# Attention, experts and MLP in one kernel: k's features shifted by a subtraction in some thirds, their maximum negated by a flag in the others, products of zeros at the start

## The chip, the core and the metric

The kernel runs on one core of a Trainium2 chip. The core has five engines with a queue of instructions each: TensorE (PE; its weight loads are listed as PEld), VectorE (DVE), ScalarE (ACT), GpSimd (POOL) and SyncE (SP, here used to issue DMAs). The metric is the device time of one launch in microseconds, the median of several runs. Three runs of the kernel before took 1137.62, 1134.53 and 1134.76 us; the median is 1134.76.

## The reference, cut to what matters

Three layers follow each other: an attention without softmax over 4 batches, 8 heads, 576 tokens and 64 columns; a mixture of 8 experts with the best 2 of each token; an MLP with a leaky ReLU. All is in 32-bit floats. The change touches only the features phi of the attention:

```python
def phi(x):                                            # q or k: (4, 8, 576, 64)
    proj = np.einsum('bhsd,df->bhsf', x, w_phi)        # (..., 128)
    proj = proj - np.max(np.abs(proj), axis=-1, keepdims=True)
    return np.concatenate([np.exp(proj), np.exp(-proj)], axis=-1)
q_p, k_p = phi(q), phi(k)
kv = np.einsum('bhsf,bhsd->bhfd', k_p, v)
num = np.einsum('bhsf,bhfd->bhsd', q_p, kv)
den = np.einsum('bhsf,bhf->bhs', q_p, k_p.sum(2))[..., None] + 1e-06
x = num / den                                          # then experts, then MLP
```

With m the largest absolute value of a row, the features are exp(proj - m) and exp(m - proj).

## The kernel before

Attention works on 16 pairs of heads (`i` from 0 to 15), one after the other. Each pair has 9 tiles of 128 rows for q and 9 for k, taken in thirds of 3 tiles (`c` = 0, 1, 2). A third goes through these steps. The raw rows are split into a high and a low 16-bit part: ScalarE makes the high part, GpSimd the low part (`split_one`, lines 303 and 304), and a DMA on SP transposes both (line 306). For the first arrays that would take too long, so `split_pe` does the split in thirds (lines 317, 318) and transposes on TensorE (line 323) with a copy by ScalarE (line 325). `proj` multiplies by w_phi into a PSUM bank `pj` (lines 333, 334). There are four such banks for all projections and transposes of both q and k; one that is asked for is waited for until its last reader is done. VectorE takes the largest absolute value of each row (line 336).

For q, VectorE then subtracts that maximum (line 343), which frees the bank; TensorE transposes the result (`q_transpose`, line 360), and ScalarE takes both exponentials of a whole third in two instructions (line 364). For k, VectorE negates the maximum (line 339), and ScalarE takes the exponentials straight from the bank with the maximum or its negative as a bias for each row. The bias is one number per partition, so there are six instructions, one per tile and sign (`k_exp`, line 352), and the bank is held until the last of them. Products of k's features with v follow (`kv`, line 374), a copy (line 382), a product that folds the routing's weights in (`fold_mm`, line 388) with its copy (line 392), and at the next pair the products with q's features (`num`, recorded at line 211).

The order is written out by hand: every engine works in the order in which the code issues. The body of the loop for pair i issues the first third of q, the last transposes of pair i-1, the first half of `kv` with half of `num` of pair i-1 between its products, then k's first third of pair i+1 and q's second; then the splits for pair i+2 and, in odd pairs, the loads for later ones; then the second half of `kv`, k's second third of pair i+1 (`proj("k", i + 1, 1)`, line 945), q's third third, the exponentials of k's second third (line 949), the fold, k's last third and its exponentials. Routing work of batches that are done is issued in small pieces in between (`flow`, `site`). Before the loop stand the splits of pair 0 and 1 and k's thirds of pair 0 (lines 826 to 854); `make_fold` puts eight copies of a unit matrix into the routing's weights for `fold_mm`. After attention come the expert products (`mm1`, line 1003, and `mm2`, line 1049) and the MLP with the same lines.

Of the kernel before, what the change touches and what calls it, by code (L numbers as in the profile page):

```python
# [7 lines left out]
F32 = mybir.dt.float32  # L8
F32R = mybir.dt.float32r
F16 = mybir.dt.float16  # L10
BF16 = mybir.dt.bfloat16
I32 = mybir.dt.int32
ACTF = mybir.ActivationFunctionType
ALU = mybir.AluOpType
AX = mybir.AxisListType.X
# [11 lines left out]
def attention_moe_mlp_kernel(  # L27
# [24 lines left out]
    nc = tc.nc  # L52
    B, H, S, D = q.shape
    F = w_phi.shape[1]
# [15 lines left out]
    const = ctx.enter_context(tc.tile_pool(name="const", bufs=1))  # L70
# [38 lines left out]
    def make_split_w_phi():  # L109
        nc.vector.tensor_scalar(out=ident, in0=iota[:, 0:128], scalar1=tokid[:, 0:1],  # L110
                                scalar2=None, op0=ALU.is_equal)
        nc.vector.tensor_copy(ident16, ident)
        nc.scalar.activation(wph, wphi, ACTF.Copy)
        nc.vector.tensor_tensor(out=wpl, in0=wphi, in1=wph, op=ALU.subtract)
# [41 lines left out]
    sm_p = att.enter_context(tc.tile_pool(name="sm", bufs=3))  # L156
# [12 lines left out]
    def make_ones(i, eng):  # L169


        eng.memset(vs[i][:, :, :, D:D + 1], 1.0)
        eng.memset(vs[i][64:128, :, 4], 0.0)
        eng.memset(vs[i][0:64, :, 9], 0.0)

    def make_pads():

        for t in qTs:
            nc.gpsimd.memset(t[:, :, :, NW:], 0.0)

    def make_fold():
        for h in range(H):
            nc.vector.tensor_copy(fr[:, h, 0:D + 1], ident[0:D + 1, 0:D + 1])
# [8 lines left out]
    ks_t = {}  # L192
    raw, stk, qT, qs_t, kvsb, fold, xb = {}, {}, {}, {}, {}, {}, {}
    nA, nB, ke = {}, {}, {}
    nb = ps_a.tile([128, 512], F32, name="nb")
# [7 lines left out]
    def pj(shape, dt, name):  # L203

        npj[0] += 1
        if npj[0] % 4 == 0:
            return ps_c.tile(shape, dt, tag="pj", name=name)
        return ps_a.tile(shape, dt, tag="pj", name=name, bufs=3)
# [82 lines left out]
    def raw_rows(nm, i):  # L291
        t = raw[nm, i // 2]
        if i % 2:
            raw.pop((nm, i // 2))
        return t[:, i % 2]

    def split_one(nm, i, eng=None, cuts=(0, NW)):

        r = raw_rows(nm, i)
        s = spl_p.tile([128, NW, 2, D], F16, tag="spl" + nm, name="spl" + nm)  # L300
        x = spl_p.tile([128, NW, 128], F16, tag="stk" + nm, name="stk" + nm, bufs=3)
        for w in map(slice, cuts, cuts[1:]):
            nc.scalar.activation(s[:, w, 0], r[:, w], ACTF.Copy)
            (eng or nc.gpsimd).tensor_tensor(out=s[:, w, 1], in0=r[:, w], in1=s[:, w, 0],
                                             op=ALU.subtract)
            nc.sync.dma_start_transpose(out=x[:, w], in_=s[:, w].rearrange("p w c d -> p (w c d)"))
        stk[nm, i] = x
# [20 lines left out]
    def proj(nm, i, c):  # L328

        x = stk[nm, i]  # L330
        p = pj([128, 3, F], F32, "pj")
        for t in range(3):
            nc.tensor.matmul(p[:, t], x[:, 3 * c + t], wpl, start=True, stop=False)
            nc.tensor.matmul(p[:, t], x[:, 3 * c + t], wph, start=False, stop=True)  # L334
        m = sm_p.tile([128, 3], F32, tag="m", name="m")
        nc.vector.tensor_reduce(out=m, in_=p, axis=AX, op=ALU.max, apply_absolute_value=True)  # L336
        if nm == "k":
            n = sm_p.tile([128, 3], F32, tag="n", name="n")
            nc.vector.tensor_scalar(out=n, in0=m, scalar1=-1.0, scalar2=None, op0=ALU.mult)
            ks_t[i, c] = p, n, m  # L340
            return
        s = sm_p.tile([128, 3, F], F32, tag="shq", name="shq", bufs=3)
        nc.vector.tensor_tensor(out=s, in0=p, in1=m.unsqueeze(2).to_broadcast([128, 3, F]),
                                op=ALU.subtract)
        qs_t[i, c] = s

    def k_exp(i, c):
        p, *shift = ks_t.pop((i, c))
        e = feat_p.tile([128, 3, 2, F], F32, tag="ke", name="ke", bufs=7)
        for t in range(3):  # L350
            for sg in range(2):
                nc.scalar.activation(e[:, t, sg], p[:, t], ACTF.Exp, scale=1.0 - 2.0 * sg,
                                     bias=shift[sg][:, t:t + 1])
        ke[i, c] = e

    def q_transpose(i, c):
        s = qs_t.pop((i, c))
        p = pj([128, 3, 128], F32, "tq")
        for t in range(3):
            nc.tensor.transpose(out=p[:, t], in_=s[:, t], identity=ident)  # L360
        if c == 0:
            qT[i] = qTs[i % 2]
        for sg in range(2):
            nc.scalar.activation(
                qT[i][:, sg, :, 3 * c:3 * c + 3].rearrange("p h w c -> p w h c"),
                p.rearrange("p w (h c) -> p w h c", h=2), ACTF.Exp, scale=1.0 - 2.0 * sg)
# [12 lines left out]
    def kv_evac(i, h):  # L379
        if h == 0:  # L380
            kvsb[i] = sm_p.tile([D + 1, 2, 2, F], F32, tag="kvs", name="kvs", bufs=2)
        nc.scalar.activation(kvsb[i][:, h], kv_of[:, :, h], ACTF.Copy)  # L382
# [333 lines left out]
    t = 0  # L716
# [102 lines left out]
        nc.vector.tensor_tensor(out=lo, in0=p, in1=hi.bitcast(F32), op=ALU.subtract)  # L819


    def take(g, n):
        for _ in range(n):
            next(g)
# [10 lines left out]
    load_q(1)  # L835
    load_v(0, 1)
    make_split_w_phi()
    make_ones(0, nc.gpsimd)
    k0 = split_pe("k", 0, nc.vector)
    take(k0, 6)  # L840
    q0 = split_pe("q", 0, nc.gpsimd)
    take(q0, 3)
    for c in range(2):
        proj("k", 0, c)
    k_exp(0, 0)
    take(q0, 1)
    k_exp(0, 1)
    take(q0, 2)
    load_gates()
    k1 = split_pe("k", 1, nc.gpsimd)  # L850
    take(k1, 3)
    split_one("q", 1)
    proj("k", 0, 2)
    make_fold()

    todo = {}

# [28 lines left out]
    for i in range(NPAIR + 1):  # L886
        nx, now, before = i + 1 < NPAIR, i < NPAIR, i > 0

        def run(place):
            for f in todo.pop((i, place), []):  # L890
                f()

        if i == NPAIR:
            att_c.close()
            ps_e = ctx.enter_context(tc.tile_pool(name="ps_e", bufs=1, space=PSUM, side="right"))
        run(0)
        first = num(i - 1, 0, 1, 2) if before else []
        second = num(i - 1, 3, 4) if before else []
        if now:
            proj("q", i, 0)  # L900
            if before:
                q_transpose(i - 1, 2)
            site(14)
            kv(i, 0, first)
            site(6, pe=True)
            kv_evac(i, 0)
            q_transpose(i, 0)
            if i == 0:
                k_exp(0, 2)
                take(k1, 3)  # L910
                split_one("k", 2)
                load_k(1, 1)
                for part in range(3):
                    load_v(1, part)
            if nx:
                proj("k", i + 1, 0)
            proj("q", i, 1)
            if nx:
                k_exp(i + 1, 0)
        else:  # L920
            for f in first:
                f()
        if before:
            x_evac(i - 1, 0)
        run(1)
        if i == 0:
            for n in range(1, NV):
                make_ones(n, nc.gpsimd)
            make_pads()
        if 0 < i < NPAIR - 2:  # L930
            split_one("k", i + 2)
        if i + 2 < NPAIR:
            split_one("q", i + 2)
        if i % 2 and (i + 3) // 2 < NPAIR // 2:
            load_double((i + 3) // 2)
        if i == 1:
            load_noise()
            make_constants()
        run(2)
        if now:  # L940
            kv(i, 1, second)
            site(3, pe=True)
            kv_evac(i, 1)
            if nx:
                proj("k", i + 1, 1)
            q_transpose(i, 1)
            proj("q", i, 2)
            if nx:
                k_exp(i + 1, 1)
            site(6)  # L950
            fold_mm(i, 0)
            fold_mm(i, 1)
            if nx:
                proj("k", i + 1, 2)
                k_exp(i + 1, 2)
            else:
                q_transpose(i, 2)
            if before:
                x_evac(i - 1, 1)
        else:  # L960
            for f in second:
                f()
        site(8, pe=True)
        run(3)
        if before:
            for d in (qT, fold):
                d.pop(i - 1)
        if now:
            for c in range(3):
                ke.pop((i, c))  # L970
# [278 lines left out]
    for bi in range(2, NB - 1):  # L1249
        s0 = steps.index((bi, 0))  # L1250
        kind, _, tiles, _ = blocks[bi + 1]
# [78 lines left out]
```

## Time and profile before

| | |
|---|---|
| median of three runs | 1134.76 us |
| the profiled execution | 1134.95 us |
| its span, first to last instruction | 1132.8 us |
| TensorE busy | 1082.2 us, 96% |
| VectorE busy | 725.4 us, 64% |
| ScalarE busy | 574.1 us, 51% |
| GpSimd busy | 219.2 us, 19% |
| granted clock of TensorE, mean | 0.993 |

All but the row of the median come from one profiled execution. Busy time is an average over parts of the run with different limits: attention takes about the first 240 us, and there all engines but SP have work; after that TensorE is busy nearly without a gap. Times in the rows are microseconds from the start of the span, and a line such as L339 is line 339 of the kernel. [...]

### The profile page before, as it was taken

The numbers are of one execution on the slowest core, as the hardware profiler recorded it, in microseconds if no ns is written. First come the engines' busy times: TensorE is split into PE (matmuls) and PEld (weight loads), VectorE is DVE, ScalarE is ACT, GpSimd is POOL, SyncE is SP. The second block draws the span as 40 slices with busy tenths as digits, with TensorE's granted clock in tenths as the row PEclk, the third lists the DMA queues.
The fourth block names the chain that finished last, engine by engine and source line by source line (L and its number), as shares of the span: only waits on it lengthen the run. The fifth ranks groups of instructions, "written<-read, shape, count | busy, mean of one in ns | idle before, by whom it ended". The sixth has DMA issues, their size and how long they took to land. (4 is left out here: it accounts for less than half of the span.)

```text
span 1132.8 us, 18373 instructions
## 1 busy us (share of the span) xinstructions
PE 1082.2 (96%) x6767; PEld 950.4 (84%) x6767; DVE 725.4 (64%) x1555; ACT 574.1 (51%) x1276; POOL 219.2 (19%) x251
## 2 busy tenths in 40 slices
PE   6999989989999999999999999889999999999998
PEld 5888988978888988888888888778888888888886
DVE  4668686878387767676667666576545645645443
ACT  6776766644455444444444454555444444444443
POOL 4211111124334315141413130330000000000000
PEclk9999999999999999999999999999999999999999
DMA  5645554634567646464546362202003003001001
GB/s 142 129 112 142 122 130 107 193 110 156 182 215 249 213 126 199 149 204 143 188 121 210 118 208 80 101 0 94 1 1 112 1 1 109 3 1 29 10 1 37
DMA packets 117003, 125.87 MB, mean 111 GB/s; under 512 B 61040, under 2 KB 87696, under 8 KB 116912
## 3 DMA queue, kind: packets, MB, share of 16 engines
q1 hardware_dynamic: 110320, 104.13, 32.0%
q0 software_dynamic: 6272, 20.03, 5.1%
q8 instruction: 54, 0.88, 0.3%
q10 hardware_dynamic: 320, 0.52, 0.1%
q14 instruction: 37, 0.30, 0.1%
HBM read 96.71 MB, written 19.40 MB: 102 GB/s over the span
## 5 line engine op out<-in xcount | busy, mean ns | idle before, releaser
L1003 PE MATMUL m<-xth,w0l 128*128 128x304 f32 (+5 forms) x800 | 268.3, 335 | 3.3 <-issue 3.3
L1003 PE MATMUL m<-xth,w0h 128*128 128x304 f32 (+5 forms) x800 | 264.9, 331 | 0.0
L1003 PE MATMUL m<-xtl,w0h 128*128 128x304 f32 (+5 forms) x800 | 264.0, 330 | 0.0
L1049 PE MATMUL o<-w1l,hh 128*128 128x512 f32 (+1 forms) x608 | 241.0, 396 | 1.7 <-POOL w1l L752 1.7
L1049 PE MATMUL o<-w1h,hh 128*128 128x512 f32 (+1 forms) x608 | 240.4, 395 | 0.0
L1049 PE MATMUL o<-w1h,hl 128*128 128x512 f32 (+1 forms) x608 | 239.5, 394 | 0.9 <-DVE hl L1007 0.9
L1003 PEld LDWEIGHTS m<-xth,w0l 128*128 128x128 f32 x800 | 150.7, 188 | 16.9 <-issue 3.7
L1003 PEld LDWEIGHTS m<-xtl,w0h 128*128 128x128 f32 x800 | 150.9, 189 | 13.8
L1003 PEld LDWEIGHTS m<-xth,w0h 128*128 128x128 f32 x800 | 150.8, 189 | 10.4
L1049 PEld LDWEIGHTS o<-w1h,hh 128*128 128x128 f32 (+1 forms) x608 | 112.8, 186 | 28.7
L1049 PEld LDWEIGHTS o<-w1h,hl 128*128 128x128 f32 (+1 forms) x608 | 113.0, 186 | 25.6 <-DVE hl L1007 1.4
L1049 PEld LDWEIGHTS o<-w1l,hh 128*128 128x128 f32 (+1 forms) x608 | 113.0, 186 | 23.8 <-POOL w1l L752 2.2
L1013 DVE SCALAR_TENSOR_TENSOR g<-g 128x512 f32<-128x512 f32 (+1 forms) x80 | 53.5, 669 | 110.5 <-ACT g L1012 110.4
L374 PE MATMUL kv<-ke,vs 128*65 128x128 f32 x640 | 121.2, 282 | 2.7 <-ACT kvs L382 1.9
L1012 ACT ACTIVATE g<-m 128x512 f32<-128x512 f32 (+1 forms) x80 | 44.4, 555 | 132.1 <-PE m L1003 131.8
L749 ACT ACTIVATE w1h<-w2r 128x512 fp32r<-128x512 f32 x88 | 55.4, 630 | 88.8 <-PE o L1049 51.1
L1007 DVE SCALAR_TENSOR_TENSOR hl<-m,hh 128x304 fp32r<-128x304 f32 (+4 forms) x128 | 57.9, 470 | 56.8 <-ACT hh L1006 56.6
L752 DVE TENSOR_TENSOR w1l<-w2r,w1h 128x512 fp32r<-128x512 f32 x72 | 49.7, 690 | 60.2 <-ACT w1h L749 59.2
L1016 DVE TENSOR_TENSOR hl<-g,hh 128x512 fp32r<-128x512 f32 (+1 forms) x80 | 51.1, 639 | 52.4 <-ACT hh L1015 49.4
L336 DVE TENSOR_REDUCE m<-pj 128x3 f32<-128x384 f32 x96 | 52.9, 551 | 48.5 <-PE pj L334 46.8
L1006 ACT ACTIVATE hh<-m 128x304 fp32r<-128x304 f32 (+4 forms) x128 | 50.5, 417 | 64.9 <-PE m L1003 62.2
L1015 ACT ACTIVATE hh<-g 128x512 fp32r<-128x512 f32 (+1 forms) x80 | 47.1, 589 | 68.4 <-DVE g L1013 68.4
(189 smaller groups left out, 1810.9 us busy)
## 6 DMA issues: line engine op xcount, KB each, us to landing
w1r<-in_moe_w_dram SPq DMA_DIRECT2D x44, 512.0 KB, 4.8
w2r<-in_moe_w_dram SPq DMA_DIRECT2D x44, 512.0 KB, 4.2
y<-y_dram SPq DMA_DIRECT2D x18, 512.0 KB, 4.9
raw<-in_moe_w_in_dram SPq DMA_DIRECT2D x16, 512.0 KB, 4.3
raw<-in_moe_w_out_dram SPq DMA_DIRECT2D x16, 512.0 KB, 3.8
rawk<-in_k_dram SPq DMA_DIRECT2D x16, 256.0 KB, 3.6
vs<-in_v_dram SPq DMA_DIRECT2D x32, 128.0 KB, 4.3
x_dram<-xb SPq DMA_DIRECT2D x4, 1024.0 KB, 5.0
```

Of the source, the lines that this page charges most:

```text
L336: nc.vector.tensor_reduce(out=m, in_=p, axis=AX, op=ALU.max, apply_absolute_value=True)
L374: nc.tensor.matmul(kv_of[:, sg, h], vs[i // 2 % NV][:, i % 2, 5 * h + n], ke[i, t // 3][:, t % 3, sg], start=(n == 0), stop=(n == 4))
L749: nc.scalar.activation(hi, src, ACTF.Copy)
L752: (nc.gpsimd if pool else nc.vector).tensor_tensor(out=lo, in0=src, in1=hi.bitcast(F32), op=ALU.subtract)
L1003: nc.tensor.matmul(p, w[:, kk], x[:, kk, c0:c1], start=(kk == 0 and m == 0), stop=(kk == KD - 1 and m == 2))
L1006: nc.scalar.activation(hh[:, c0:c1], p, ACTF.Relu)
L1007: nc.vector.scalar_tensor_tensor(out=hl[:, c0:c1], in0=p, scalar=0.0, in1=hh[:, c0:c1].bitcast(F32), op0=ALU.max, op1=ALU.subtract)
L1012: nc.scalar.activation(g, p, ACTF.Copy)
L1013: nc.vector.scalar_tensor_tensor(out=g, in0=g, scalar=0.01, in1=g, op0=ALU.mult, op1=ALU.max)
L1015: nc.scalar.activation(hh[:, c0:c1], g, ACTF.Copy)
L1016: nc.vector.tensor_tensor(out=hl[:, c0:c1], in0=g, in1=hh[:, c0:c1].bitcast(F32), op=ALU.subtract)
L1049: nc.tensor.matmul(acc[n][0:rows], a[:, c], w, start=(f == 0 and m == 0), stop=(f == nf - 1 and m == 2))
```

## The change

Three things change in the attention part, and nothing behind it.

- For k, the thirds of pairs 0 and 1 and the second third of every later pair now go the way of q: VectorE subtracts the maximum into a tile in SBUF (`shk`, two buffers), and ScalarE takes the exponentials of the whole third from there in two instructions. The first and last third of pairs 2 to 15 keep their six exponentials, but the negated maximum is made by a maximum over one element with the negate flag, in place of a multiplication by -1.
- A tile of zeros, 128 by 512 in 16 bits, is filled by VectorE at the start, and TensorE multiplies zeros by zeros: nine products ahead of the first transposes and five more, one or two at a time, before the loop. They write into the bank `nb`, which the first pair's results use only later.
- `make_fold` moves from before the loop to behind the exponentials of k's last third of pair 0, and the transposes of pair 1's k move from there to ahead of the first transposes of q.

```diff
         nc.vector.tensor_reduce(out=m, in_=p, axis=AX, op=ALU.max, apply_absolute_value=True)
-        if nm == "k":
+        if nm == "k" and i > 1 and c != 1:
             n = sm_p.tile([128, 3], F32, tag="n", name="n")
-            nc.vector.tensor_scalar(out=n, in0=m, scalar1=-1.0, scalar2=None, op0=ALU.mult)
+            nc.vector.tensor_reduce(out=n, in_=m.unsqueeze(2), axis=AX, op=ALU.max, negate=True)
             ks_t[i, c] = p, n, m
             return
-        s = sm_p.tile([128, 3, F], F32, tag="shq", name="shq", bufs=3)
+        s = sm_p.tile([128, 3, F], F32, tag="sh" + nm, name="sh" + nm, bufs=3 if nm == "q" else 2)
         nc.vector.tensor_tensor(out=s, in0=p, in1=m.unsqueeze(2).to_broadcast([128, 3, F]),
                                 op=ALU.subtract)
-        qs_t[i, c] = s
+        if nm == "q":
+            qs_t[i, c] = s
+        else:
+            ks_t[i, c] = s,
...
         p, *shift = ks_t.pop((i, c))
         e = feat_p.tile([128, 3, 2, F], F32, tag="ke", name="ke", bufs=7)
-        for t in range(3):
+        for sg in () if shift else range(2):
+            nc.scalar.activation(e[:, :, sg], p, ACTF.Exp, scale=1.0 - 2.0 * sg)
+        for t in range(3) if shift else ():
             for sg in range(2):
...
+    zeros = const.tile([128, 512], BF16, name="zeros")
+
+    def warm(n):
+
+        for _ in range(n):
+            nc.tensor.matmul(nb, zeros[:, 0:128], zeros, start=True, stop=True)
+
...
     make_split_w_phi()
+    nc.vector.memset(zeros, 0.0)
+    warm(9)
     make_ones(0, nc.gpsimd)
     k0 = split_pe("k", 0, nc.vector)
...
     k_exp(0, 0)
+    warm(1)
     take(q0, 1)
     k_exp(0, 1)
+    warm(1)
     take(q0, 2)
     load_gates()
     k1 = split_pe("k", 1, nc.gpsimd)
     take(k1, 3)
     split_one("q", 1)
+    warm(2)
     proj("k", 0, 2)
-    make_fold()
+    warm(1)
...
             kv_evac(i, 0)
+            if i == 0:
+                take(k1, 3)
             q_transpose(i, 0)
             if i == 0:
                 k_exp(0, 2)
-                take(k1, 3)
+                make_fold()
```

## Rows read from the trace of the kernel before

**Rows 1.** The page's part 4: the chain that ended last, by line
```profile
PE m L1003 16%; PE o L1049 16%; PE t L815 1%; DVE y L794 1%; ACT w0h L749 0%; DVE g L1013 0%; DVE w0l L752 0%; DVE xtl L819 0%; ACT w1h L749 0%; ACT xth L818 0%; DVE xg L797 0%; DVE yo L1054 0%; ACT yo L1056 0%; ACTq L1063 0%; ACT hh L1015 0%
```

**Rows 2.** What TensorE waited for, 28 to 240 us: total, times, longest
```profile
PE pj L333 <- ACT ke L352: 7.7, 6, 1.7
PE tq L360 <- ACT ke L352: 2.2, 2, 1.4
PE pj L333 <- DVE shq L343: 1.9, 3, 0.8
...
PE tq L360 <- DVE n L339: 1.7, 1, 1.7
PE tq L360 <- DVE shq L343: 1.5, 3, 0.7
PE pt L656 <- DVE hot L648: 1.2, 1, 1.2
```

**Rows 3.** Timeline of VectorE around one end of a pair: start, us, what
```profile
65.55 0.56 DVE L336 TENSOR_REDUCE m<-pj 128x3 f32<-128x384 f32 x1 [1.31 <-PE pj L334]
66.14 1.28 DVE L339 TENSOR_SCALAR n<-m 128x3 f32<-128x3 f32 x1
67.33 0.54 DVE L336 TENSOR_REDUCE m<-pj 128x3 f32<-128x384 f32 x1
67.91 0.56 DVE L343 TENSOR_TENSOR shq<-pj,m 128x384 f32<-128x384 f32 x1
68.39 0.55 DVE L336 TENSOR_REDUCE m<-pj 128x3 f32<-128x384 f32 x1
```

**Rows 4.** Instructions of lines 339, 343: ns min/median/max, first and last start
```profile
L339 DVE TENSOR_SCALAR n<-m x48: 168/169/1321, 7.9 to 223.5; 128x3 f32<-128x3 f32 x48
L343 DVE TENSOR_TENSOR shq<-pj,m x48: 556/557/559, 13.3 to 234.5; 128x384 f32<-128x384 f32 x48
```

**Rows 5.** Timeline of GpSimd, two of its splits
```profile
12.85 1.56 POOL L318 TENSOR_TENSOR splk<-rawk,splk 128x192 f16<-128x192 f32 x3 [1.48 <-ACT splk L317]
...
66.11 1.28 POOL L304 TENSOR_TENSOR splq<-rawq,splq 128x576 f16<-128x576 f32 x1
```

**Rows 6.** Timeline of TensorE at the same end of a pair
```profile
69.16 0.22 PE L333 MATMUL pj<-wpl,stkq 128*128 128x128 f16 x1 [1.74 <-ACT ke L352]
...
69.49 0.50 PE L360 MATMUL tq<-ident,shq 128*128 128x128 f32 x3
```

**Rows 7.** Stretches: us; PE, PEld, DVE, ACT, POOL busy (count); PEclk, DMA, GB/s
```profile
12.40:16.90 4.50, 4.50 (x24) 4.50 (x23) 1.38 (x5) 1.44 (x5) 2.79 (x4) 1.00 0.45 99
16.90:20.30 3.40, 1.18 (x14) 0.87 (x13) 0.00 (x0) 3.35 (x11) 0.00 (x0) 1.00 0.46 87
20.30:23.70 3.40, 3.40 (x24) 3.40 (x23) 2.64 (x4) 1.85 (x6) 2.00 (x6) 0.51 0.02 5
163.70:166.70 3.00, 1.52 (x20) 1.40 (x18) 2.93 (x8) 2.56 (x9) 1.19 (x1) 1.00 0.64 122
166.70:170.50 3.80, 3.80 (x25) 3.80 (x24) 3.28 (x15) 2.65 (x9) 0.00 (x0) 0.56 0.34 63
```

**Rows 8.** Timeline of ScalarE after the first kv
```profile
17.33 0.87 ACT L364 ACTIVATE qT<-tq 128x384 f32<-128x384 f32 x2
18.09 0.37 ACT L352 ACTIVATE ke<-pj,n 128x128 f32<-128x128 f32 x1
...
19.58 1.30 ACT L325 ACTIVATE stkk<-tr 128x384 f16<-128x384 f16 x3
```

**Rows 9.** Timeline of TensorE at the start
```profile
5.33 1.14 PE L323 MATMUL tr<-ident,splk 128*128 128x128 f16 x9 [5.33 <-DVE splk L318]
...
12.40 4.47 PE L374 MATMUL kv<-ke,vs 128*65 128x128 f32 x20
...
24.70 0.22 PE L333 MATMUL pj<-wpl,stkk 128*128 128x128 f16 x1
```

**Rows 10.** Groups by line, VectorE: count, busy us, mean ns, idle before
```profile
L119 DVE MEMSET ones<- 128x128 bf16 x1 | 0.2, 165 | 0.0
```

## The prediction

> **What bounds the kernel now.** I read the chain of waits first. [rows 1] There the reader is to see that the chain that ends last is TensorE nearly throughout and lies in the two expert and MLP products, lines 1003 and 1049. The change touches nothing there: it can only let that stretch begin earlier or later, so every microsecond won or lost in the attention stretch (the first 240 us) goes through to the end. So I next asked what TensorE waits for inside attention. [rows 2] These six rows add up to 7.7 + 2.2 + 1.9 + 1.7 + 1.5 + 1.2 = 16.2 us between 28 and 240 us. Almost all of it stands at one place, once in each head pair: the end of the pair, where pair i hands over to pair i+1. The timeline of one such place [rows 3] shows why, on VectorE: the maximum of k's second third begins at 65.55, its negation takes 1.28 us for three numbers per partition, and q's maximum and subtraction, and k's last third, queue behind it. Over all 48 negations the median is 169 ns and the longest 1321 ns [rows 4]. The long ones are those that start beside a GpSimd split: here the split of q runs from 66.11 to 67.39 and the negation ends at 67.42 [rows 5]. TensorE pays twice [rows 6]: the first projection of the next pair waits 1.74 us (69.16) for the bank that ScalarE's six exponentials of that third still read, and the transposes of q's last third follow at 69.49. At the start a third view matters, the stretches by granted clock [rows 7].
>
> **Second third of k by subtraction (pairs 2 to 15, 14 handovers).** Removed: a negation and six exponentials from PSUM. Added: one subtraction on VectorE and two exponentials of 384 columns. The subtraction's price is that of q's, 556 to 559 ns in all 48 [rows 4]; in a queue the next instruction starts about 0.08 us before it has ended, so it takes 0.48. A maximum takes 0.56 and its successor starts 0.58 after it. So the new handover is: k's maximum, subtraction, q's maximum, subtraction = 0.58 + 0.48 + 0.58 + 0.56, plus 0.06 until TensorE starts: q's transposes start 2.26 us after k's maximum. The bank of k is free after 0.58 + 0.56, before the next pair's first projection wants it (TensorE's own work from its projection of k to q's transposes takes about 2.6 us from 0.54 us before the maximum, so 2.06 us after it, and 2.26 ends last). In [rows 3, 6]: 65.55 + 2.26 = 67.81 instead of 69.49, a gain of 1.68. What is late next there is VectorE's subtraction of q, by 0.2 us, not a bank.
>
> The same subtraction for every handover, each from the start of the maximum of k's second third to the start of q's transposes: 39.77 to 42.26 (gain 0.23), 52.31 to 55.29 (0.72), 65.55 to 69.49 (1.68), 79.49 to 82.41 (0.66, and 0.36 that TensorE then waits for the fold copy, which comes earlier with ScalarE's shorter work: 1.02), 93.74 to 96.98 (0.98), 121.97 to 124.95 (0.72), 135.21 to 138.73 (1.26), 150.28 to 153.19 (0.65), 163.31 to 166.99 (1.42), 179.21 to 182.84 (1.37), 193.46 to 196.98 (1.26), 207.13 to 210.12 (0.73), 220.23 to 223.36 (0.87); of these 13 pairs of rows one stands, in [rows 3, 6]. At 108.03 routing work stands between: there the two table rows on VectorE end 0.71 earlier, and I count 0.71. Sum 13.6 us. The upper end is the whole of [rows 2], less the 0.4 at 28 us and 0.5 at 235 us that are no such handover: 15.3. The lower end: if the subtraction too were held until GpSimd's split ends, it would start when the negation now ends; q's subtraction would end 0.47 later than now, and the same list gives 3.0. I take 13.6, since the 48 subtractions show no long one, the first of them (13.30 us) beside GpSimd's splits from 12.85 [rows 4, 5].
>
> [...]
>
> **The negate flag (first and last thirds).** The negation becomes a maximum over one element each. No such row exists; the bounds are 169 ns of the old form and 540 ns of a maximum over 128 columns [rows 4, 3], and I take 0.17, as start-up cost makes up most of both for so few numbers. These thirds have their negation at the median, clear of GpSimd; no wait goes and none comes: 0. If it cost 0.54, the last third's sits behind q's subtraction, off TensorE's path, and ScalarE would begin it 0.4 later, with the fold copy in front of it already done. So 0 in both cases.
>
> **ScalarE.** Two exponentials of 384 columns cost as q's pair, 0.87 [rows 8]; six cost 1.5 (18.09 to 19.58). That is 0.6 us per third, 12 us over 20 thirds, but TensorE sees it only through banks and the fold copy, which are counted above, and through the start, below.
>
> [...]
>
> **The start.** The zero fill stands on VectorE ahead of k's split, and the first nine zero products on TensorE ahead of the first transposes, which began at 5.33 [rows 9]. The fill is four times the 128-column memset of 165 ns [rows 10] at most, 0.66; the products can then start at about 5.4, where the split's end put the transposes. [...] From there to the first kv it was 7.07 us, nearly all ScalarE in one chain; k's first two thirds take 4 x 0.435 there instead of 12 x 0.25, 1.26 less, and the projections at full clock 0.3 less: kv starts at 14.75. In front of it stand five more zero products, hidden while ScalarE is the chain. It is half as long if the clock is up, 2.24, and ends at 17.0, against 16.87 now; if the clock isn't up, the projections and fillers take 1.25 more and it ends at 20.4. Is it up? [...] I take it as up.
>
> After the first kv, now: copy of kv, q's pair, six exponentials, three copies of the next k, and k's second third of pair 1 is projected at 24.70 [rows 8, 9], 7.83 after kv's end. New: copy 0.4, three copies 1.3, q's pair 0.87, half a pair of exponentials, then the rest of the second kv, which waits for them: 4.15. Of the 3.7 us won, 1.7 is the clock, which is 0.51 in 20.3 to 23.7 now [rows 7]. The fold's copies move behind all this on VectorE and are needed 2 us later. The start gains 24.70 - 21.15 = 3.55 if the clock holds. It fell now after 16.9 to 20.3 with TensorE busy 1.18 of 3.40 us, and after 163.7 to 166.7 with 1.52 of 3.00 [rows 7]. New it is busy some 1.5 of 3 after the first kv, like the second of these rows, so I take one more fall, half of 3.4 us: 1.7. The start is worth 1.85, with ends 3.55 and, with the clock not up and a fall behind it, a loss of 1.55.
>
> **The fall at 166.7.** The 1.5 us gap in front of it is one of the handovers that close. 3.8 us at 0.56 lose 1.65 [rows 7]; it should go. Ends 0 and 1.65; I take 1.65, because with a 0.2 us gap that stretch looks like the others, at 1.00.
>
> **Sum.** 13.6 + 1.85 + 1.65 = 17.1. The profiled execution took 1134.95 (span 1132.8 and 2.15 around it), 0.2 above the median shown: 1134.95 - 17.1 = 1117.85, and I predict 1117.8.
>
> **Rivals.** (1) Half of the handover gain turns into a new wait: the loads of the pair after next, which SP issues at the handovers, come in at the same time while ScalarE's split comes 1.7 us earlier. For it: six handovers carry such loads. Against: no ScalarE wait for a load among the rows, and q's load lands about 1.3 us before the earlier split would ask. It gives 1134.95 - 6.8 - 1.85 = 1126. Chance 0.14. (2) The change doesn't do what it says, and the subtraction is held like the negation: handovers 3.0, start and fall nothing: 1132. Against it the 559 ns. Chance 0.07. (3) The zeros don't raise the clock: 13.6 + 1.65 - 1.55 = 13.7, 1121; for it, that only real products have raised it in the trace. Chance 0.10. (4) Slower: the late start is never paid back. [...] Chance 0.04. The forecast keeps 0.65, with its own range 1113 to 1124 (15.3 and both clock terms at their best at one end; 11 and no clock term at the other).
>
> **Range and chances.** A change under 0.3%, 3.4 us, can't be told from none. Faster by more needs under 1131.4: forecast, (1), (3) and a part of (2), 0.92; same 0.04; slower 0.04. The range 1112 to 1129 takes in (1) and (3) and leaves out (2) and (4).
>
> **What would show it.** Right: no negation of k above 0.2 us after the first pairs; waits of TensorE at projections and q's transposes between 28 and 240 us down from 16 to about 3; the handover 2.3 us from k's maximum to q's transposes; attention ending some 17 us earlier and the rest unchanged. Wrong: subtractions of 1 us; TensorE's first kv ending after 18; a new releaser at the handovers; clock of 0.5 between 17 and 24 twice.

## The result and the profile after

The changed kernel took 1118.0 us (median of 4 runs, 1117.33 to 1120.06), the kernel before beside it 1136.19 us (4 runs, 1134.53 to 1137.89). The ratio is 0.9843, with a 95% interval of 0.9819 to 0.9866: 1.6% faster. The profiled execution took 1117.33 us with a span of 1115.3, so against the profiled execution of before the difference is 17.6 us in time and 17.5 in span.

The chain that ended last is still TensorE in the two expert and MLP products (lines 1022 and 1068 are 1003 and 1049 of before), as in [rows 1]:

```profile
PE m L1022 17%; PE o L1068 16%; PE t L820 1%; DVE y L799 1%; ACT w0h L754 0%; DVE g L1032 0%; DVE w0l L757 0%; DVE xtl L824 0%; ACT w1h L754 0%; ACT xth L823 0%; DVE xg L802 0%; DVE yo L1073 0%; ACTq L1082 0%; ACT yo L1075 0%; ACT hh L1034 0%
```

What TensorE waited for between 26 and 230 us of the kernel after (total, times, longest), which answers to [rows 2]:

```profile
PE kv L379 <- ACT kvs L387: 3.3, 2, 2.2
PE tq L365 <- DVE shq L343: 2.8, 3, 1.4
PE pt L661 <- DVE hot L653: 1.0, 2, 0.5
PE o L1068 <- DVE hl L1026: 0.9, 1, 0.9
```

The reader is to see that the two rows on `ke` (7.7 and 2.2 us), the row on `n` and the projections' row on `shq` are gone: no bank of k is waited for any more. The first two rows that are left stand at a few pairs each; the first is the subject of kernels e5 and e6.

VectorE at the end of the pair that [rows 3] showed, in the kernel after (start, us, what):

```profile
60.07 0.56 DVE L336 TENSOR_REDUCE m<-pj 128x3 f32<-128x384 f32 x1 [1.38 <-PE pj L334]
60.66 0.56 DVE L343 TENSOR_TENSOR shk<-pj,m 128x384 f32<-128x384 f32 x1
61.14 0.55 DVE L336 TENSOR_REDUCE m<-pj 128x3 f32<-128x384 f32 x1
61.72 0.56 DVE L343 TENSOR_TENSOR shq<-pj,m 128x384 f32<-128x384 f32 x1
```

TensorE's transposes of q's last third follow at 62.42, 2.35 us after the first row (before: 65.55 to 69.49, 3.94). Four rows of instructions with their durations (ns min/median/max), where [rows 4] had the old ones: the sign change, k's new subtraction, k's new exponential, which reads SBUF, and beside it q's, which reads PSUM:

```profile
L339 DVE TENSOR_REDUCE n<-m x28: 155/156/157, 30.3 to 208.7; 128x3 f32<-128x3 f32 x28
...
L343 DVE TENSOR_TENSOR shk<-pj,m x20: 557/557/558, 10.9 to 205.6; 128x384 f32<-128x384 f32 x20
...
L354 ACT ACTIVATE ke<-shk x40: 506/522/543, 11.5 to 206.6; 128x384 f32<-128x384 f32 x40
...
L369 ACT ACTIVATE qT<-tq x96: 470/491/537, 17.8 to 220.2; 128x384 f32<-128x384 f32 x96
```

TensorE at the start, which answers to [rows 9]:

```profile
5.23 3.81 PE L832 MATMUL nb<-zeros 128*128 128x512 bf16 x9 [5.23 <-DVE zeros L850]
8.88 0.67 PE L323 MATMUL tr<-ident,splk 128*128 128x128 f16 x9
...
14.01 2.35 PE L379 MATMUL kv<-ke,vs 128*65 128x128 f32 x20
...
21.12 0.22 PE L333 MATMUL pj<-wpl,stkk 128*128 128x128 f16 x1
```

The nine transposes took 0.67 us here and 1.14 before, and ahead of them TensorE had nothing but products of zeros: so in this run these zeros alone had brought the clock to its upper level.

The stretches after the first kv, and the one that answers to the fall at 166.7 in [rows 7]; the columns are those of that group, and the granted clock stands third from the end:

```profile
16.20:19.60 3.40, 2.78 (x33) 2.09 (x31) 3.30 (x11) 3.21 (x9) 1.36 (x2) 1.00 0.26 44
19.60:23.00 3.40, 3.40 (x37) 3.38 (x38) 2.03 (x5) 3.08 (x8) 2.53 (x10) 1.00 0.34 70
...
155.30:159.10 3.80, 3.66 (x39) 3.52 (x36) 3.77 (x18) 2.37 (x9) 0.00 (x0) 1.00 0.75 141
```

All three are at 1.00, that is at the upper level. A third fall of before, which the prediction did not list, is gone too; the row is of before, and no stretch of after between 9 and 700 us is below 1.00:

```profile
269.40:273.00 3.60, 3.60 (x15) 3.02 (x13) 2.06 (x10) 1.94 (x4) 0.66 (x1) 0.53 0.04 9
```

**Where the 17.5 us of span came from.** The marks are the starts of the transposes of q's last third, 16 in each kernel. The first came at 27.81 before and at 23.98 after: 3.83 us at the start. The last came at 235.18 and 219.23, so the 15 stretches between two marks gave 12.12 us more; 1.65 of it is the clock at 166.7 ([rows 7]), which leaves 10.47 to the handovers. After the attention 1.55 us are left, about half of the 3.4 us that before spent at the lower clock from 269.5 on. This compares one execution with one. The start of kernel e1 below differs from that of before only in the flag, and with another course of the clock it is some 2.5 us shorter; so the 3.83 at the start are not all shown to be the change's.

### The profile page after: what moved, and what is told of

It reads as the page before. It is cut to its first block, busy times and chain, and to the rows that moved or that the text cites. A ratio compares the mean times of both kernels' runs of the same rounds, so it can differ in the third digit from the quotient of the medians.

```text
span 1115.3 us, 18305 instructions
## 1 busy us (share of the span) xinstructions
PE 1077.4 (97%) x6781; PEld 943.9 (85%) x6781; DVE 725.0 (65%) x1556; ACT 559.8 (50%) x1196; POOL 220.1 (20%) x251
## 5 line engine op out<-in xcount | busy, mean ns | idle before, releaser
L1022 PEld LDWEIGHTS m<-xth,w0l 128*128 128x128 f32 x800 | 150.9, 189 | 16.9 <-issue 3.7
L379 PE MATMUL kv<-ke,vs 128*65 128x128 f32 x640 | 117.4, 273 | 4.0 <-ACT kvs L387 3.3
```

The source lines that it names most:

```text
L379: nc.tensor.matmul(kv_of[:, sg, h], vs[i // 2 % NV][:, i % 2, 5 * h + n], ke[i, t // 3][:, t % 3, sg], start=(n == 0), stop=(n == 4))
L1022: nc.tensor.matmul(p, w[:, kk], x[:, kk, c0:c1], start=(kk == 0 and m == 0), stop=(kk == KD - 1 and m == 2))
```

## The experiments

The kernels ran in three groups of four, each group on one chip beside the kernel before, which took 1134.15, 1134.85 and 1134.68 us (medians of 9 to 11 runs).

### 1 and 2: the sign change alone, the subtraction alone

Kernel e1 is the kernel before with the flag in all 48 sign changes and nothing else:

```
-            nc.vector.tensor_scalar(out=n, in0=m, scalar1=-1.0, scalar2=None, op0=ALU.mult)
+            nc.vector.tensor_reduce(out=n, in_=m.unsqueeze(2), axis=AX, op=ALU.max, negate=True)
```

> The kernel before with one line changed: all 48 negations by the negate flag, six exponentials kept, no zeros, no move. Theory (the hold of the negation by GpSimd is what costs): no negation above 0.2 us; VectorE is through 0.4 to 1.1 us earlier at 12 handovers, but at 9 of them the bank is still held by six exponentials of 1.5 us, so 0.5 to 0.9 us is won per handover, of which some 2.5 us go to longer waits elsewhere: about 6.5 us in all, 1128.5 (1126 to 1131). Rival (the six exponentials that hold the bank are what costs, whenever they begin): under 2 us, 1133 or more.

Measured: 1126.38 us (6 runs, 1123.74 to 1127.38), ratio 0.992 (0.99 to 0.9939). Line 339 of e1, and what its TensorE waited for between 26 and 230 us:

```profile
L339 DVE TENSOR_REDUCE n<-m x48: 155/156/157, 8.0 to 213.4; 128x3 f32<-128x3 f32 x48
```

```profile
PE pj L333 <- ACT ke L352: 5.6, 6, 1.0
PE kv L374 <- ACT fold L392: 1.9, 4, 0.6
PE kv L374 <- ACT kvs L382: 1.8, 2, 1.2
```

None of the 48 is held any more, at the same places beside GpSimd's splits where the multiplication took up to 1321 ns [rows 4]. The time is inside the range that was expected. But the bank of k is still waited for, 5.6 us of the 7.7: six exponentials read it. By the marks the handovers gave 5.57 us.

The profiled execution of e1 took 1123.78 us, one of the two shortest of its six, and its span is 11.1 us under that of before. The falls of the clock at 166.7 and 269.5 are gone in it too (its mean granted clock is 0.998 for 0.993), and its first mark is at 24.96 against 27.81, though up to there it differs from the kernel before only in the flag:

```profile
12.48 3.65 PE L374 MATMUL kv<-ke,vs 128*65 128x128 f32 x20
...
22.21 0.22 PE L333 MATMUL pj<-wpl,stkk 128*128 128x128 f16 x1
```

```profile
20.30:23.70 3.40, 3.40 (x38) 3.25 (x36) 2.24 (x7) 3.22 (x11) 2.67 (x11) 1.00 0.18 37
```

In the kernel before these were 4.47 us at 12.40, 24.70, and a granted clock of 0.51 in the same stretch ([rows 7, 9]). Here the clock rose inside the first kv, near 15.1 (an estimate from its 3.65 us, between 4.47 at the lower and 2.35 at the upper clock), and not by 16.9 as there; it did not fall again, so 24.70 became 22.21 without any change to the start but the flag.

Kernel e2 is the kernel before with the subtraction in the second third of pairs 2 to 15, and the old multiplication in all other thirds:

```
+        if nm == "k" and not (i > 1 and c == 1):
             n = sm_p.tile([128, 3], F32, tag="n", name="n")
             nc.vector.tensor_scalar(out=n, in0=m, scalar1=-1.0, scalar2=None, op0=ALU.mult)
```

> The kernel before with only the second third of pairs 2 to 15 by subtraction; old negation elsewhere, no zeros, no move, start as before. Theory: the handovers are worth 10.5 us as in the trace of after, and the fall of the clock behind 166.7 may go too: 1122.5 to 1124.5; first kv still ends at 16.9, pair 1's second third of k is still projected near 24.7. Rival (the start and the flag carry the gain): 1130 or more.

Measured: 1121.05 us (4 runs, 1118.55 to 1121.45), ratio 0.9867 (0.9843 to 0.9891). Its handovers gave 10.20 us by the marks, the change's 10.47. That is 1.5 us under the range that was expected, and its trace has no fall of the clock at 166.7 (granted clock 1.00 from 26 to 230 us, where that of before, with the fall, has 0.99). Its start is that of before: the lower clock is back there at 20.43 (products of one projection 0.11 us apart, 0.06 from 24.79 on), and the first mark stands at 27.99. So the subtraction does nearly all that the handovers give, and the flag in the other thirds does next to nothing on top of it, as predicted; the flag in its place gives about half (e1). What the rest of the change adds to e2 is, by the two ratios (0.9867 and 0.9843), some 2.7 us, with intervals that overlap.

### 3 and 4: without the zeros, and with the zeros first

Kernel e3 is the kernel after without the products of zeros (and their fill); e4 has the fill as VectorE's first instruction and the nine products as TensorE's first:

```
-    nc.vector.memset(zeros, 0.0)
-    warm(9)
...
-    warm(1)
...
```

```
+    nc.vector.memset(zeros, 0.0)
+    warm(9)
...
     load_k(0, 0)
...
     make_split_w_phi()
-    nc.vector.memset(zeros, 0.0)
-    warm(9)
```

> The changed kernel without the zero fill and the fourteen products of zeros. [...] Theory B (what they win in clock they cost in delay, and ScalarE's shorter chain made the start): first transposes at 5.3, first kv from 11.1 to 15.5, second third of pair 1's k near 21 as now, within 1.5 us of the changed kernel, 1117 to 1119.5.

> The changed kernel with the zero fill as VectorE's first instruction and the nine products ahead of all else on TensorE. If the zeros raise the clock and cost only by standing in front of the transposes: they run from about 0.6 to 4.4 us, the transposes start at 5.3 instead of 8.9, everything behind is 3.5 us earlier, 1114.5. [...]

Measured: e3 1115.04 us (5 runs, 1113.42 to 1115.78), ratio 0.9824 (0.9804 to 0.9843); e4 1114.78 us (5 runs, 1113.52 to 1116.39), ratio 0.9821 (0.9801 to 0.9841). Both are some 3 us under the kernel after, or 2.2 by the ratios, whose intervals overlap with that of the kernel after; the theory on e3 (1117 to 1119.5) did not have this, while e4 is near the 1114.5 that was expected if the zeros only stood in the way. The start of e3 on TensorE:

```profile
5.49 1.14 PE L323 MATMUL tr<-ident,splk 128*128 128x128 f16 x9 [5.49 <-DVE splk L318]
...
10.38 2.35 PE L379 MATMUL kv<-ke,vs 128*65 128x128 f32 x20
```

The transposes run 3.4 us earlier than in the kernel after, and the first kv takes 2.35 us, that is at the upper clock, without one product of zeros. So the nine products, put in front of the transposes, moved the start back by what they take, for a clock that this start had anyhow in this trace. Whether it always has it was left to the last four kernels.

### 5 and 6: the route's exponential behind its tables

In the kernel after, ScalarE around TensorE's longest wait of the attention, and that wait:

```profile
136.22 0.21 ACT L676 ACTIVATE ex<-dm 128x5 f32<-128x5 f32 x1 [3.17 <-DVE dm L672]
136.33 0.36 ACT L387 ACTIVATE kvs<-kv 65x256 f32<-65x256 f32 x1
```

```profile
136.74 0.43 PE L379 MATMUL kv<-ke,vs 128*65 128x128 f32 x2 [2.19 <-ACT kvs L387]
```

In ScalarE's queue `ex` stands first: it starts at 136.22, after 3.17 us of waiting for VectorE's routing chain (`dm`), and the copy `kvs` that TensorE wants starts behind it, at 136.33. Kernel e5 is the kernel after, e6 the kernel without zeros, each with the route's weights behind its tables in all blocks:

```
-            late = self.b > 1
+            late = True
```

> The kernel after, with one thing moved: in the first two blocks of the route too, the exponential of the weights (ex) is issued behind the tables, not ahead of the ranks. Theory A: the 3.1 us that the handovers gave less than predicted are TensorE's two waits for ScalarE's copy kvs (1.16 us at 81.87 and 2.19 at 136.74), for ScalarE stands in order behind ex, which waits 2.87 and 3.17 us for VectorE's routing chain (dm). Then both waits go: 1118.0 less 3.35, 1114.7 us (1114 to 1116). Theory B (rival): VectorE itself is late at these two handovers, since the routing chain stands ahead of the maxima; then taking ex away only changes the name of the wait, 1117 to 1119 us.

> The kernel after without the products of zeros, and with ex behind the tables in every block. Theory A (the two gains lie in different places, the first 21 us and the two handovers, and add up): 1115.0 less 3.35, 1111.7 us (1110.8 to 1113). Rival: less activity on TensorE in either place brings back a fall of the clock, which costs some 1.6 us each: 1113.5 to 1115.5.

Measured: e5 1115.07 us (5 runs, 1114.02 to 1118.25), ratio 0.9822 (0.98 to 0.9844); e6 1110.55 us (5 runs, 1110.28 to 1112.84), ratio 0.9787 (0.9767 to 0.9808). What TensorE of e6 waited for between 26 and 230 us:

```profile
PE tq L365 <- DVE shq L343: 1.9, 2, 1.4
...
PE kv L393 <- ACT kvs L387: 0.9, 2, 0.5
```

The row of kv on `kvs` (3.3) is gone, for 0.9 on it at the fold's product; the stretch between two marks that held the long wait is 13.02 us in e6 and 14.76 in e3. All 15 stretches together are 3.2 us shorter in e5 than in the kernel after, and 2.9 shorter in e6 than in e3. Theory A holds for the cure. It does not hold as the account of my error: of the 3.35 us of the two waits 1.86 stood at the same places in the kernel before (0.52 and 1.34).

### 7: the old order at the start

Kernel e7 is e3 with the order of before at the start:

```
     proj("k", 0, 2)
+    make_fold()
...
-            if i == 0:
-                take(k1, 3)
             q_transpose(i, 0)
             if i == 0:
                 k_exp(0, 2)
-                make_fold()
+                take(k1, 3)
```

> The kernel after without the products of zeros and with the old order at the start (k's transposes of pair 1 behind q's transposes and k_exp, make_fold ahead of the loop); the subtraction in all thirds of pairs 0 and 1 stays. Theory A (ScalarE's shorter chain, two exponentials of 0.52 us for six, makes the start): the first kv still begins near 10.4 us with the clock up, and only the wait of k(1)'s projections for its transposed copy comes back, 1.6 us: 1116.6 us (1115.5 to 1118). Rival B (the order makes it): the start is as in the kernel before, with the late rise and the second fall of the clock, and the time is that of the subtraction alone in pairs 2 to 15: 1119.5 to 1122 us.

Measured: 1116.41 us (5 runs, 1116.16 to 1117.83), ratio 0.9832 (0.9813 to 0.9851), inside theory A's range; but the clock rose only inside the first kv, which took 3.41 us: near 12.9, by the same estimate as for e1. Two of its first waits on TensorE:

```profile
PE tq L365 <- DVE shq L343: 1.7, 1, 1.7
PE pj L333 <- ACT stkk L325: 1.7, 1, 1.7
```

The predicted wait for k's transposed copy is back, and a second one with it: VectorE now copies the fold's pieces ahead of q's subtraction. These copies take longer than before, too. The first row is of e7, where GpSimd's splits stand beside them from 11.62 to 14.42, the second of the kernel before, where the next split began at 12.85, behind them:

```profile
11.47 3.21 DVE L183 COPY fr<-ident 65x65 f32<-65x65 f32 x8
```

```profile
11.77 0.90 DVE L183 COPY fr<-ident 65x65 f32<-65x65 f32 x8
```

The first mark is at 24.30 (before 27.81, e1 24.96, e3 20.41). So ScalarE's shorter chain is worth 3.5 us there against the trace of before, but only 0.7 against that of e1, whose clock rose inside the first kv and did not fall again, as in e7. The order is worth up to another 3.9, of which some 1.8 is the early clock that only e3 had here and some is the copies' longer time; the medians differ by 1.4 us.

### 8: subtraction in all thirds

Kernel e8 is e3 with `if False:` in place of `if nm == "k" and i > 1 and c != 1:`, and three buffers for the differences.

> The kernel after without the products of zeros, and with VectorE's subtraction in all three thirds of k in every pair: 28 more subtractions of 0.557 us for 28 sign changes of 0.157 on VectorE (11.2 us more, 154 to 165 of 204 us busy), and for ScalarE 168 exponentials of 0.376 become 56 of 0.515 (34 us less). Theory A (TensorE bounds the attention, and the projection's banks are free as soon as VectorE has subtracted): no handover gets longer, and of the waits only those for ScalarE get shorter: 1114 us (1112.5 to 1116). Rival B (VectorE in order is the bound at the handovers: its extra 0.4 us per third lands in front of the next maximum): 0.4 to 0.8 us in each of 14 pairs, 1120 to 1126 us.

Measured: 1124.16 us (6 runs, 1120.82 to 1127.1), ratio 0.9889 (0.987 to 0.9909): rival B. What its TensorE waited for, and two stretches of it:

```profile
PE tq L365 <- DVE shq L343: 6.7, 12, 1.6
PE kv L379 <- ACT kvs L387: 4.3, 2, 2.7
PE pt L661 <- DVE hot L653: 2.7, 2, 2.1
```

```profile
105.70:109.00 3.30, 3.30 (x20) 3.30 (x19) 2.38 (x9) 1.32 (x4) 0.00 (x0) 0.50 0.02 5
139.80:143.20 3.40, 3.32 (x17) 3.32 (x18) 3.27 (x8) 2.75 (x7) 1.15 (x1) 0.51 0.00 0
```

But the price is not in every pair, as rival B had it. By the marks, pairs without routing work became 0.07 us longer (12.47 for 12.40, 12.44 for 12.37, 12.35 for 12.28), and the seven with it 0.8 to 2.1 us longer each, 10.5 in all; two of these hold a fall of the clock, half of 3.4 us, so 7 us are VectorE's. VectorE was busy 165.8 of the 204 us against 157.1. The traced execution was the longest of the six (1127.1 us). Of the two choices that were run, one third of three is the better: VectorE has room for one subtraction of k per pair, not for three.

### 9 to 12: zeros and late weights on one chip

The last four kernels are the kernel after (f1), e3 again (f2), the zeros first as in e4 with the late weights (f3), and e6 again (f4).

> The kernel after itself, run beside the next three on one chip, so that they can be compared with one another and not only through the kernel before. 1118 us (1116.5 to 1120).

> The kernel after without the products of zeros. Theory A (the nine zeros in front of the first transposes cost their 3.5 us, and the clock rises without them): 3 us under the kernel after of the same chip, 1115 us. Theory B (the difference seen before came from one start in which the clock happened to rise early): within 1 us of the kernel after. In its trace the first kv, of 20 products, takes 2.35 us if the clock has risen by then and 3.4 or more if it has not; it took 2.35 in two and 3.63 in one of the three traces that have this start.

> Nine products of zeros as TensorE's first work, in time in which it would stand idle, five more in later gaps, and ex behind the tables in every block. Theory A (zeros that cost nothing make the early rise of the clock certain): the first kv takes 2.35 us, and the time is that of the next kernel or up to 1 us under it. Theory B (they add nothing to a start in which the clock rises early by itself, and their later five stand in the way): the same to 1 us over it.

> No products of zeros, and ex behind the tables in every block: the two gains together, on the chip of the kernel after. If they add up, 6 to 7.5 us under the kernel after, 1111 to 1112 us, and 3 to 4.5 under the kernel without zeros alone; if the second was noise, under 1.5.

| kernel | median us (5 runs) | lowest to highest | ratio to before (95%) | first kv: start, us | first mark |
|---|---|---|---|---|---|
| f1, after | 1117.58 | 1117.39 to 1120.65 | 0.9857 (0.9836 to 0.9879) | 14.43, 2.35 | 24.40 |
| f2, no zeros | 1115.72 | 1113.38 to 1117.02 | 0.983 (0.9808 to 0.9852) | 10.88, 3.76 | 22.27 |
| f3, zeros first, late weights | 1110.6 | 1110.52 to 1113.3 | 0.9794 (0.9774 to 0.9815) | 10.40, 2.35 | 20.37 |
| f4, no zeros, late weights | 1113.08 | 1112.35 to 1113.5 | 0.9806 (0.9787 to 0.9826) | 10.71, 3.75 | 22.08 |

The first kv of f2 and of f3, the second with the nine zero products ahead of it:

```profile
10.88 3.76 PE L379 MATMUL kv<-ke,vs 128*65 128x128 f32 x20
```

```profile
1.18 4.02 PE L832 MATMUL nb<-zeros 128*128 128x512 bf16 x9 [1.18 <-DVE zeros L834]
5.24 0.88 PE L323 MATMUL tr<-ident,splk 128*128 128x128 f16 x9
...
10.40 2.35 PE L379 MATMUL kv<-ke,vs 128*65 128x128 f32 x20
```

Of theory A on f3 the early clock holds in these traces, and its gain over f4 was larger than the 1 us expected. On f2 neither theory came out: it is 1.9 us under f1, and its clock was not up at the first kv. f4 is 4.5 us under f1 and 2.6 under f2, short of the 6 to 7.5 and 3 to 4.5 that were expected if the gains add up. Without zeros the same start has two outcomes: the clock is up at the first kv (e3 and e6, 2.35 us, first mark 20.4) or rises inside it (e8, f2 and f4, 3.6 to 3.8 us, first mark 22.1 to 22.3). In all five traces with zeros (after, f1, e4, e5, f3) the first kv took 2.35 us. So zeros do bring the early clock, worth 1.6 to 1.9 us at the first mark; where the change puts them they cost 3.5 to do it. That they bring it each time is likely from five traces against two of five, no more. The intervals of f1 and f2 overlap, and those of f2 and f4, so these sizes are rough; f4 and f1 are apart. f3 is 7.0 us under f1, with intervals apart: it beats both kernels, 2.1% under the kernel before. Against f4, 2.5 us slower, the intervals overlap too, though their five runs hardly do.

## Why the prediction was right, step by step

The time was forecast at 1117.8 us and came out at 1118.0. The mechanism was right; that the sum fits this closely is owed to three terms whose errors cancel: the handovers 3.1 us too large, the start 1.7 to 2.0 too small, and a fall of the clock of 1.5 that was not counted. That is luck, and so is part of the start: the execution of before that the sum starts from had a late rise and a second fall there, which e1 has not.

**Handovers, 13.6 predicted, 10.47 measured.** Right: the subtraction is not held (557 to 558 ns in all 20), the bank is free in time, and the new handover is the predicted chain of two maxima and two subtractions (2.35 us for 2.26). Of the 14 listed handovers nine came out within 0.2 us of their number, two were off by +0.55 (the first; in e2, with the start of before, it is the predicted 0.23) and -0.38 (the fourth), and three failed, by 1.10, 0.96 and 0.90 us. That is 2.96 of the 3.13 missing. The formula was applied to these three as if nothing but k and q stood on VectorE and ScalarE before them; at each of them routing work does.

- The stretch that ends at 103.85 (predicted gain 0.71, measured a loss of 0.39). The handover itself gained what was said: 3.24 us from k's maximum to the transposes, 3.94 before. The loss lies inside the pair, where TensorE's table products now come while VectorE is still at the rows they need. The first row is of the kernel after, the second of before:

```profile
93.93 1.63 PE L661 MATMUL pt<-hot 128*128 128x144 f32 x4 [0.47 <-DVE hot L653]
```

```profile
101.74 1.24 PE L656 MATMUL pt<-hot 128*128 128x144 f32 x4
```

  Before, the same four waited for nothing; 0.47 + 1.63 - 1.24 = 0.86 of the 1.10. The pair begins earlier on TensorE, while VectorE has as much to do in it as before. This is read from the two traces; no kernel here tests it.

- The stretch that ends at 143.34 (0.65, measured -0.31): the wait for `kvs` behind `ex`, shown above, grew from 1.34 to 2.19 us, 0.85 of the 0.96. Kernels e5 and e6 confirm it: the whole wait goes with `ex`.

- The handover at 194.92 (0.73, measured -0.17). VectorE of the kernel after, and GpSimd beside it:

```profile
191.63 1.12 DVE L594 TENSOR_TENSOR oh<-oh,re 128x64 f32<-128x64 f32 x1
192.68 0.54 DVE L336 TENSOR_REDUCE m<-pj 128x3 f32<-128x384 f32 x1
```

```profile
191.39 1.28 POOL L304 TENSOR_TENSOR splk<-rawk,splk 128x576 f16<-128x576 f32 x1 [10.80 <-ACT splk L303]
```

  The product of the routing in front of k's maximum took 0.23 us before and 1.12 here; the 0.89 are as much as is missing. The last section follows this hold through four traces.

**The start, 1.85 predicted, 3.58 measured** (24.70 to 21.12 at the projection of k's second third of pair 1). The parts were right: the zeros made the transposes 3.55 us late (8.88 for 5.33), kv began at 14.01 (14.75) and took 2.35 us (2.24). The 14.75 has 3.9 us in it for the nine products ahead of the transposes, a term that no run had shown; here the nine took 3.81. That the clock would be up at kv was my estimate; the 0.67 us of the nine transposes and the 2.35 of kv show it for this run. What failed is the fall of the clock put after it: TensorE was busy 2.78 of the 3.40 us after the first kv, not half. What I did not price is the alternative: with the same shorter chain and no zeros in front, the gain at the first mark is 5.5 to 7.4 us (e3, f2). All these gains are counted from the one trace of before. Counted from e1, whose projection stood at 22.21, the start gave 1.1 us; how much of the 3.58 belongs to the change stays open between these two.

**The fall at 166.7, 1.65 predicted**: gone, as said. The one at 269.5, outside the stretch that I looked at, went with it. That the closed gap is the cause is not shown: both are gone in e1 as well, where TensorE still waits 0.93 us at that handover, and before's longer gap at 69.16 (1.74 us) was followed by no fall.

**The negate flag, 0 predicted**: 156 ns for the 0.17 taken. A maximum over 384 numbers per partition takes 549 ns, so by these two times (an estimate) its three numbers make up some 3 ns of the 156, and the rest is start-up. And e2, which lacks it, has handovers that differ by 0.27 in all. **ScalarE's pair from SBUF, 0.87 predicted**: two of 0.522 where q's take 0.491.

Each of these, which reads SBUF, is 31 ns longer at the median than one of q's, which reads PSUM. The two also write tiles of different layout, so the share of the source is not measured by itself.

**Rivals.** No load became a new wait (1); no subtraction took more than 559 ns (2); the clock rose, and on zeros alone (3; the nine transposes behind them took 0.67 us for 1.14). The lower end of 3.0 counted the twelve handovers with a held negation and left out the 0.23 and 0.87 of the other two, so by that list it is 4.1. The fourth did not come: the transposes were 3.55 us late, but the start as a whole gained 3.58, and the handovers returned 10.47.

## What to carry to other kernels

An instruction that goes from a queue does not only shorten that queue: every other instruction behind it meets the other engines' work at another time (here 0.47 us more of waiting at 93.93 and 0.89 more of the hold at 191.63), so list what stands beside each in the new time line, the routing rows too, and not only the ones that the edit touches. A filler that is to bring the clock up belongs into time in which the engine would stand idle; put in front of the first real work it cost 3.5 of its 3.8 us here. Where a queue has a wait for a long chain ahead of a copy that the bound engine needs, move the wait: on one chip that gave 2.6 us here (f4 against f2).

## What was not expected of the hardware

The hold beside GpSimd's split went from one VectorE instruction to another. In the row at 191.63 above a product of 64 columns takes 1.12 us and ends 0.08 us behind GpSimd's split; at the same place before, where GpSimd's split ended 0.1 us after it began, it took 0.23. Four traces give its size against the stretch up to the next mark: 1.12 us and 13.31 (after), 1.11 and 13.31 (e3), 0.85 and 13.04 (e2), 0.22 and 12.83 (e6). From the first to the third the stretch moves by just what the hold does; in e6 other waits of that stretch changed too. Both inputs of this one are in SBUF. The multiplication by -1, with one input, was held too (up to 1321 ns in [rows 4]), while the flag's maximum, also with one, was never held in 48 (157 ns at most, e1). Which instructions are held, and by what, is not shown beyond these.

The clock's rise at the start is not fixed by the program: with the same instructions up to there the products of a projection stood 0.06 us apart from 9.8 us on in two traces (e3, e6) and 0.11 apart up to the first kv, at 10.7 to 11.0, in three (e8, f2, f4), where that kv took 3.63 to 3.76 us. What decides between them, and why falls stood near 231 to 249 us in some of these kernels (granted clock 0.52 from 231.0 to 234.5 in e3) and not in others (1.00 there in e6), stays open; no kernel here was made to tell it.
